# Three orders changed in a two-layer MLP behind a Fourier layer: weight sums by a written plan, output sums over three iterations, VectorE's PSUM sums first

## The chip, the cores and the metric

The kernel runs on one core of a Trainium2 chip. The metric is the device time in microseconds (us). The engines are TensorE (PE, with PEld for its weight loads), VectorE (DVE), ScalarE (ACT), GpSimd (POOL) and SyncE (SP), whose queue issues the transfers that matter here. Each engine takes its own instructions in program order; semaphores order the engines against one another.

## The reference

A Fourier layer gives 6016 tokens of 256 numbers; two MLP layers follow, and their weights are `moe_` and `moe2_`:

```python
def reference(...):
    x = attn_out.reshape(B * S, D)          # rfft, complex matmul, soft threshold, irfft
    h = x @ w_in;  g = h * (1.0 / (1.0 + np.exp(-h)));  x = g @ w_out      # layer 1, d_ff 2048
    h = x @ w_in2; g = np.maximum(0.01 * h, h);         return g @ w_out2  # layer 2
```

## The kernel before

Numbers are float32, and TensorE works on rounded ones, so each operand is split: ScalarE copies the *high* part, VectorE or GpSimd subtracts it from the source to get the *low* part, and one product is three matmuls (low weight x high data, high x low, high x high).

The MLP runs over 12 chunks of tokens (11 of 512, one of 384) for layer 1 and the same 12 for layer 2. Within a chunk, eight iterations take one pair of 128 hidden units each. An iteration of the main loop works on three pairs in turn: `pr` (its first matmul), `one` (the pair before: its activation's parts are made) and `two` (the pair before that: its products with `w_out` are added up in PSUM, in four banks `acc(0)` to `acc(3)`).

Most pairs run "in blocks", a seven-product scheme for a 2x2 block product in place of eight. It needs sums of weight blocks, and sums of data blocks: `t1` (GpSimd), `t23` and `t4` (VectorE) make sums of the activation. The parts are `"1"` (`high`: h, `low`: l), `"a"` (ha, la; la on GpSimd) and `"b"` (hb, lb). At the end of a chunk the four banks are summed into two output tiles (`close`, or `finish` outside the quick chunks) and stored by SP. The first layer has the scheme for `w_out` only. In layer 2 the chunks 2 to 10 are *quick*: there the product with `w_in` too has seven products (`seven(k)`, three matmuls of 256 columns each), whose results `keep`, `join(0)` and `join(1)` put together in PSUM (px and py, four banks in turn, two per iteration). A quick iteration has 42 matmuls of 256 columns; `quick_turn` writes out its order by hand. The data sums of the next quick chunk (tsum, and the parts B11, B21, T1 to T4, B22) are made one step an iteration, from the third on (`ahead_quick`, `make_next`); in the last iteration of a chunk two steps are made.

Between the layers, weights are exchanged. The last chunk of layer 1 (the short one) and the chunks 0 and 1 of layer 2 are the 24 iterations that are called *the tail* here, numbered 0 to 23 from the variable `tail`. In them, `next_in` splits `w_in` of layer 2 for each pair, `sums_w2` makes four sums of `w_out` blocks a pair on GpSimd (128x128 each), which `split_w` splits in the next iteration, and `sum_in` takes three iterations a pair: GpSimd adds the high and low parts of `w_in` together again (128x512), VectorE makes four sums of 128x128, and then the sums are split. Three lists of iterations say when:

```python
SEVENS_AT = [9, 12, 15, 16, 17, 18, 19, 20]
IN_AT, SUMS_AT = [1, 3, 4, 6, 7, 9, 10, 12], [3, 5, 6, 8, 10, 11, 13, 14]
```

All of this stands at the end of the iteration, after `one.high("b")` and `one.low("b")`. In a quick iteration VectorE's order is t23, t4, low "1", join 0, join 1, (closing sums), low "b".

Of the kernel before, what the change touches and what calls it, by code (L numbers as in the profile page):

```python
# [9 lines left out]
F32 = mybir.dt.float32  # L10
F32R = mybir.dt.float32r
# [69 lines left out]
def spectral_mlp_kernel(ctx, tc, x, w_r, w_i, b_r, b_i, w_in1, w_out1, w_in2, w_out2, da, ea, dm, out):  # L81
# [349 lines left out]
    big = pool("big", 1, side="right", **near)  # L431
    m4 = pool("m4", 2, side="right", **near)
    ring = [big.tile([128, 2, RING], F32R, name=f"x{p}") for p in parts]
    place = lambda layer, c: CHUNKS[c][0] % RING if layer == 1 or c < 2 else 512
    at = lambda t: t % RING
    quick = lambda layer, c: layer == 2 and 2 <= c < len(CHUNKS) - 1
    accs, x2f, late = {}, {}, {}

    def inverse(h, c):
# [44 lines left out]
    def sum_x2(c, second):  # L484
        x = [x2f[c][h][:, t * 256:(t + 1) * 256] for h in range(2) for t in range(2)]
        if not second:
            sums_x[c] = [stage.tile([128, 512], F32, tag="wraw", name="tsum", bufs=2) for _ in range(2)]
        t1, t2, t3, t4 = (u[:, k * 256:(k + 1) * 256] for u in sums_x[c] for k in range(2))
        for d, a, b in ((t2, x[3], t1), (t4, x[2], t2)) if second else ((t1, x[1], x[0]), (t3, x[3], x[1])):
            nc.gpsimd.tensor_tensor(out=d, in0=a, in1=b, op=ALU.subtract)  # L490

# [7 lines left out]

    def ahead_quick(c):  # L500
        pool_, x = nc.gpsimd, lambda h, a, b: x2f[c][h][:, a:b]
        return [[lambda: load_x2(c)], [],
                [lambda: sum_x2(c, False), lambda: split_b(c, B22, 1, x(1, 256, 512), pool_)],
                [lambda: sum_x2(c, True)],
                [lambda: split_b(c, T1, 2, sums_x[c][0], pool_), lambda: split_b(c, T3, 2, sums_x[c][1], nc.vector)],
                [lambda: [split_b(c, k, 1, x(h, 0, 256)) for h, k in enumerate((B11, B21))]],
                [lambda: [split_b(c, k, 1, x(h, 0, 256), nc.vector, False) for h, k in enumerate((B11, B21))]]]

    made = [0]

# [45 lines left out]
    def sums_w2(p):
        sums_w(p, m_out[p // 4][:, p % 4 * 512:][:, :512])

    def next_in(p):

        src, hi, lo = (w[:, :, p % 4 * 256:][:, :, :256] for w in [m_in[p // 4]] + [w_in[p // 4][q] for q in parts])
        nc.scalar.copy(hi, src)
        nc.vector.tensor_tensor(out=lo, in0=src, in1=hi.bitcast(F32), op=ALU.subtract)

    sums_in = []

    def sum_in(p):
        if p % 4 == 0:
            sums_in.append({q: homes[p // 4].tile([128, 4, 4, 128], F32R, tag=f"hold{k}", name=f"s{q}") for k, q in enumerate(parts)})
        t = btp.tile([128, 1024], F32, tag="bt", name="wsum")  # L570
        r, s = t[:, :512].rearrange("p (h e) -> p h e", h=2), t[:, 512:].rearrange("p (i e) -> p i e", i=4)
        hi, lo = (w_in[p // 4][q][:, :, p % 4 * 256:][:, :, :256].bitcast(F32) for q in parts)
        nc.gpsimd.tensor_tensor(out=r, in0=hi, in1=lo, op=ALU.add)
        yield
        a = [r[:, h, u * 128:(u + 1) * 128] for u in range(2) for h in range(2)]
        for d, x, y, op in ((s[:, 0], a[2], a[3], ALU.add), (s[:, 2], a[0], a[2], ALU.subtract),
                            (s[:, 1], s[:, 0], a[0], ALU.subtract), (s[:, 3], a[1], s[:, 1], ALU.subtract)):
            nc.vector.tensor_tensor(out=d, in0=x, in1=y, op=op)  # L578
        yield
        hi, lo = (sums_in[p // 4][q][:, p % 4] for q in parts)  # L580
        nc.scalar.copy(hi, s)  # L581
        nc.vector.tensor_tensor(out=lo, in0=s, in1=hi.bitcast(F32), op=ALU.subtract)

    class Pair:

# [156 lines left out]
                    self.product(self.acc(i)[:, :self.n], wh[w], wl[w], hi, lo, b, e)  # L742

        def close(self):
            if self.p != NF // 2 - 1:
                return [lambda: None] * 4
            tt, g = nc.vector.tensor_tensor, nc.gpsimd.tensor_tensor
            half = lambda a, k: a[:, k * 256:(k + 1) * 256]
            both = lambda a: a.rearrange("p (k n) -> p k n", k=2)
            twice = lambda a: a.rearrange("p (k n) -> p k n", k=1).to_broadcast([128, 2, 256])  # L750
            acc = [self.acc(i) for i in range(4)]
            o = [stage.tile([128, 512], F32, tag="wraw", name="x2o", bufs=2) for _ in range(2)]
            u = stage.tile([128, 256], F32, tag="wc", bufs=4, name="u")
# [9 lines left out]
            def third():
                nc.scalar.copy(u, half(acc[2], 0))
                tt(out=half(o[0], 1), in0=half(o[0], 1), in1=half(acc[2], 0), op=ALU.add)
                tt(out=u, in0=u, in1=half(acc[2], 1), op=ALU.add)

            def fourth():
                tt(out=half(o[1], 1), in0=half(o[1], 1), in1=half(acc[3], 0), op=ALU.subtract)
                g(out=half(o[0], 0), in0=half(o[0], 0), in1=u, op=ALU.add)  # L770
                g(out=both(o[1]), in0=both(o[1]), in1=twice(u), op=ALU.add)
# [3 lines left out]
            return [first, second, third, fourth]  # L775

        def finish(self, part):
            if self.p != NF // 2 - 1:
# [52 lines left out]
    SEVENS_AT = [9, 12, 15, 16, 17, 18, 19, 20]  # L831
    IN_AT, SUMS_AT = [1, 3, 4, 6, 7, 9, 10, 12], [3, 5, 6, 8, 10, 11, 13, 14]

    def make_next():
        if todo and (make := todo.pop(0)):
            make()

    sevens = []

    def quick_turn(pr, one, two, i):  # L840
        last = pr.p == NF // 2 - 1
        if pr.p == 2:
# [36 lines left out]
        sp[6]()
        pr.seven(4)  # L880
        pr.unit(0)
        pr.t1()
        closing[2]()
        closing[3]()
        if not last:
            make_next()

    for i in range(len(pairs) + 2):
# [74 lines left out]
        if k <= i <= NF:  # L963
            split_w()
            if i < NF:
                sums_w1(i - k)
        elif i < tail:
            if i == NF + 1:
                for home in homes:
                    m_in.append(home.tile([128, DFF], F32, tag="hold0", name="m_in").rearrange("p (d c) -> p d c", d=2))  # L970
                    m_out.append(home.tile([128, DFF], F32, tag="hold1", name="m_out"))
                _, step_w, _, _ = weight_pieces(w_in2, w_out2, lambda k: [m_in[k]], lambda k: [m_out[k]], 1)
            if i > NF and i % 2 == 0:
                step_w()
        else:
            split_w()
            if i - tail in IN_AT:
                next_in(IN_AT.index(i - tail))
            if i - tail in SUMS_AT:
                sums_w2(SUMS_AT.index(i - tail))  # L980
            if i - tail in SEVENS_AT:
                sevens.append(sum_in(SEVENS_AT.index(i - tail)))
            for steps in list(sevens):
                if next(steps, sevens) is sevens:
                    sevens.remove(steps)


# [25 lines left out]
```

## Time and profile before

| | |
|---|---|
| median of 3 runs | 1172.87 us (1170.99 to 1173.26) |
| profiled execution | 1171.28 us, span 1169.5 us |
| granted TensorE clock | 1.000 of full speed |
| busy share of the span | PE 98%, PEld 91%, DVE 71%, ACT 72%, POOL 55% |

The span runs from the first to the last instruction; about 1.8 us of the profiled time lie around it. Busy shares are averages over stages that have different limits, so the stages are to be read one by one.

### The profile page before, as it was taken

How to read it: one execution, taken by the hardware profiler on the slowest of the kernel's cores; microseconds unless marked ns; L12 is line 12 of the kernel's file. 1: busy time of each engine (PE TensorE's matmuls, PEld its weight loads, DVE VectorE, ACT ScalarE, POOL GpSimd, SP SyncE). 2: the span in 40 equal slices, each digit the busy share in tenths (PEclk: the TensorE clock that was granted, in tenths of full speed). 3: DMA queues.
4: the chain of work that ended last, by engine and by line, in shares of the span. 5: the costliest groups of instructions: out<-in, count | busy, mean ns of one | idle time of the engine just before them, and what ended most of it. 6: DMA issues, size and time to landing. Idle time of an engine off the chain costs nothing.

```text
span 1169.5 us, 21790 instructions
## 1 busy us (share of the span) xinstructions
PE 1140.8 (98%) x7932; PEld 1062.5 (91%) x7932; DVE 835.2 (71%) x1543; ACT 843.9 (72%) x1801; POOL 638.9 (55%) x693
## 2 busy tenths in 40 slices
PE   9999999999999999999999988789999999999998
PEld 9889988889999999999999976689999999999998
DVE  4898865455666666666665688888788778877863
ACT  4788876666666666667666765578888888888884
POOL 0567746444454454544544675546756665666552
PEclk9999999999999999999999999999999999999999
DMA  9345532010111210111100001010111011001000
GB/s 245 115 135 160 166 122 91 14 50 19 57 53 41 64 59 28 59 50 35 46 29 27 17 26 36 1 37 2 37 37 37 2 37 37 13 25 38 32 3 31
DMA packets 36187, 61.84 MB, mean 53 GB/s; under 512 B 3952, under 2 KB 16080, under 8 KB 36080
## 3 DMA queue, kind: packets, MB, share of 16 engines
q1 hardware_dynamic: 35792, 60.28, 16.5%
q8 instruction: 62, 1.02, 0.3%
q14 instruction: 45, 0.37, 0.1%
q10 hardware_dynamic: 288, 0.18, 0.1%
HBM read 41.83 MB, written 18.61 MB: 52 GB/s over the span
## 4 chain that ended last, share of the span: by engine, by line
PE 79%; DVE 12%; ACT 4%; issue 3%; POOL 2%; DVEq 0%; POOLq 0%
PE acc L709 30%; PE ph L636 24%; PE px L612 6%; PE pz L332 6%; PE py L612 4%; PE py L361 3%; PE pa L284 3%; PE px L446 2%; DVE u L683 2%; DVE wsum L578 2%; PE pb L384 1%; DVE l L664 1%; DVE lb L664 1%; DVE u L621 1%; DVE u L690 1%
## 5 line engine op out<-in xcount | busy, mean ns | idle before, releaser
L664 POOL TENSOR_TENSOR la<-u,ha 128x512 fp32r<-128x512 f32 (+1 forms) x176 | 226.2, 1286 | 172.9 <-ACT ha L702 172.9
L664 DVE TENSOR_TENSOR lb<-u,hb 128x768 fp32r<-128x768 f32 (+1 forms) x176 | 177.1, 1006 | 155.5 <-ACT hb L702 155.3
L676 POOL TENSOR_TENSOR u<-u 128x256 f32<-128x256 f32 x160 | 139.4, 871 | 84.5 <-ACT u L627 61.5
L702 ACT CAST hb<-u 128x768 fp32r<-128x768 f32 (+1 forms) x176 | 141.8, 806 | 59.1 <-DVE u L690 58.1
L636 PE MATMUL ph<-xhi,winhi 128*128 128x512 f32 (+1 forms) x480 | 143.6, 379 | 0.0
L636 PE MATMUL ph<-xlo,winhi 128*128 128x512 f32 (+1 forms) x480 | 143.4, 379 | 0.0
L636 PE MATMUL ph<-xhi,winlo 128*128 128x512 f32 (+1 forms) x480 | 143.2, 379 | 0.0
L709 PE MATMUL acc<-lb,whi 128*128 128x256 f32 (+1 forms) x496 | 138.6, 279 | 4.6 <-DVE lb L664 4.6
L709 PE MATMUL acc<-hb,wlo 128*128 128x256 f32 (+1 forms) x496 | 137.8, 278 | 0.0
L709 PE MATMUL acc<-hb,whi 128*128 128x256 f32 (+1 forms) x496 | 137.6, 277 | 0.0
L702 ACT CAST ha<-u 128x512 fp32r<-128x512 f32 (+1 forms) x176 | 110.8, 629 | 2.1 <-PE acc L709 1.9
L659 ACT ACTIVATE ph<-ph 128x512 f32<-128x512 f32 (+1 forms) x112 | 64.7, 577 | 63.8 <-PE ph L636 63.8
L709 PE MATMUL acc<-l,whi 128*128 128x256 f32 (+1 forms) x336 | 94.3, 281 | 11.0 <-DVE l L664 11.0
L636 PEld LDWEIGHTS ph<-xhi,winhi 128*128 128x128 f32 x480 | 89.5, 187 | 15.9
L636 PEld LDWEIGHTS ph<-xlo,winhi 128*128 128x128 f32 x480 | 89.4, 187 | 15.7
L709 PE MATMUL acc<-ha,wlo 128*128 128x256 f32 (+1 forms) x352 | 99.3, 282 | 0.5 <-ACT shi L581 0.4
L709 PEld LDWEIGHTS acc<-lb,whi 128*128 128x128 f32 x496 | 93.1, 188 | 6.3 <-DVE lb L664 6.3
L709 PE MATMUL acc<-la,whi 128*128 128x256 f32 (+1 forms) x352 | 98.8, 281 | 0.0
L709 PE MATMUL acc<-ha,whi 128*128 128x256 f32 (+1 forms) x352 | 98.7, 280 | 0.0
L709 PE MATMUL acc<-h,wlo 128*128 128x256 f32 (+1 forms) x336 | 94.9, 282 | 1.6 <-ACT x2o L785 1.6
L659 ACT ACTIVATE u<-ph 128x512 f32<-128x512 f32 (+1 forms) x80 | 47.0, 588 | 67.0 <-PE ph L636 65.1
L683 DVE TENSOR_TENSOR u<-px,u 128x512 f32<-128x512 f32 x72 | 49.7, 690 | 63.7 <-ACT h L702 42.2
(176 smaller groups left out, 3584.0 us busy)
## 6 DMA issues: line engine op xcount, KB each, us to landing
wraw<-in_moe_w_in_dram SPq DMA_DIRECT2D x32, 256.0 KB
wraw<-in_moe_w_out_dram SPq DMA_DIRECT2D x32, 256.0 KB
scr<-bo SPq DMA_DIRECT2D x48, 128.0 KB
scr<-x2o SPq DMA_DIRECT2D x22, 256.0 KB
x2i<-scr SPq DMA_DIRECT2D x22, 256.0 KB
out_dram<-x2o SPq DMA_DIRECT2D x22, 256.0 KB
dmr<-in_dm_dram SPq DMA_DIRECT2D x34, 160.0 KB
bt<-scr SPq DMA_DIRECT2D x14, 384.0 KB
```

Source lines behind the costliest of these rows:

```text
L284: nc.tensor.matmul(pa[h][:, s * 128:(s + 1) * 128], lhsT=xt[c][:, s, h * 128:(h + 1) * 128], rhs=da_sb, start=True, stop=True, skip_group_ ...
L332: nc.tensor.matmul(turned(pz), lhsT=u[:, h, :], rhs=turned(v[:, h].rearrange("p g e -> p (g e)")), start=(n == 0), stop=(n == len(terms) - 1))
L361: nc.tensor.matmul(turned(py), lhsT=u, rhs=turned(v), start=False, stop=(n == len(terms) - 1), skip_group_check=True)
L446: nc.tensor.matmul(px[:, s * PAIR:(s + 1) * PAIR], lhsT=bt[:, s, h * 128:(h + 1) * 128], rhs=ea_sb, start=True, stop=True, skip_group_chec ...
L612: nc.tensor.matmul(turned(out), lhsT=x, rhs=turned(y), start=(k < 3 and i == 0), stop=(i == 2), skip_group_check=True)
L636: nc.tensor.matmul(turned(ph), lhsT=u[:, h, f % HALF * 128:][:, :128], rhs=turned(v[:, h, :]), start=(i == 0), stop=(i == len(terms) - 1))
L659: nc.scalar.activation(out=out, in_=ph, func=ACTF.Silu)
L664: eng.tensor_tensor(out=lo, in0=src, in1=hi.bitcast(F32), op=ALU.subtract)
L676: nc.gpsimd.tensor_tensor(out=blk(1), in0=blk(0), in1=blk(2), op=ALU.subtract)
L683: nc.vector.tensor_tensor(out=v[:, 3:5], in0=b22, in1=v[:, 0:2], op=ALU.subtract)
L702: nc.scalar.copy(hi, src)
L709: nc.tensor.matmul(turned(dst), lhsT=u, rhs=turned(v), start=(begin and self.p == 0 and i == 0), stop=(end and self.p == NF // 2 - 1 and i ...
```

## The change

- The weight exchange follows one table, `PLAN`: generators that do a step each time they are called, with the iterations (from -6 to 23) in which they step. `sums_w2`, `next_in` and `sum_in` take two pairs at once (256 columns an instruction where there were 128). `sum_in` reads the unsplit weights `m_in`, makes all its sums on GpSimd, and the splits follow later in `split_in`. `plan` is called behind the products and ahead of `one.high("b")`.
- `close` has seven parts in place of four: one ScalarE copy more (both halves of `acc(2)`), VectorE adds two PSUM halves fewer into other tiles, GpSimd has two sums more; and the parts are spread over iterations 1, 2 and 3 of the next chunk, with the store at the end of iteration 3.
- In `quick_turn`, `one.low("1")` goes behind `join(0)` and `join(1)`; the order of `two`'s products that was used in the closing iteration is now used in all.
- In `ahead_quick`, T1 to T4 are split one by one (256 columns), T1 and T3 an iteration earlier; in a chunk's last iteration B11 is made (both parts) behind `keep(2)`, ahead of `high("a")`, and B21 behind `join(1)`, ahead of `low("1")`.

```diff
     def sum_x2(c, second):
...
-            sums_x[c] = [stage.tile([128, 512], F32, tag="wraw", name="tsum", bufs=2) for _ in range(2)]
+            sums_x[c] = [stage.tile([128, 256], F32, tag="wc", name="tsum", bufs=4) for _ in range(4)]
...
     def ahead_quick(c):
...
+        t = lambda k, eng: split_b(c, k, 1, sums_x[c][k - T1], eng)
         return [[lambda: load_x2(c)], [],
                 [lambda: sum_x2(c, False), lambda: split_b(c, B22, 1, x(1, 256, 512), pool_)],
-                [lambda: sum_x2(c, True)],
-                [lambda: split_b(c, T1, 2, sums_x[c][0], pool_), lambda: split_b(c, T3, 2, sums_x[c][1], nc.vector)],
-                [lambda: [split_b(c, k, 1, x(h, 0, 256)) for h, k in enumerate((B11, B21))]],
-                [lambda: [split_b(c, k, 1, x(h, 0, 256), nc.vector, False) for h, k in enumerate((B11, B21))]]]
+                [lambda: sum_x2(c, True), lambda: t(T1, pool_), lambda: t(T3, nc.vector)],
+                [lambda: t(T2, pool_), lambda: t(T4, nc.vector)],
+                [lambda: split_b(c, B11, 1, x(0, 0, 256), nc.vector)], [lambda: split_b(c, B21, 1, x(1, 0, 256), nc.vector)]]
...
+    def sums_w2(k):
+        b = m_out[k // 2][:, k % 2 * 1024:][:, :1024].rearrange("p (j i e) -> p i j e", j=2, i=4)
...
+            nc.gpsimd.tensor_tensor(out=d, in0=x, in1=y, op=op)
+            yield
...
+        for i, n, u in ((A11, 1, src[:, :, :1]), (A12, 2, src[:, :, 2:]), (S1, 2, t[0]), (S3, 2, t[1])):
+            hi, lo = (late[q][:, 2 * k:2 * k + 2, i:i + n] for q in parts)
+            nc.scalar.copy(hi, u)
+            nc.vector.tensor_tensor(out=lo, in0=u, in1=hi.bitcast(F32), op=ALU.subtract)
+            yield
...
+    def sum_in(k):
+        src = m_in[k // 2][:, :, k % 2 * 512:][:, :, :512].rearrange("p h (j u e) -> p j u h e", j=2, u=2)
...
+            nc.gpsimd.tensor_tensor(out=d, in0=x, in1=y, op=op)
+            yield
...
+            return [first, second, third, fifth, fourth, sixth, seventh]
...
+    PLAN = [(sum_in(0), [-6, -5, -4, -1]), (sums_w2(0), [-3, -3, -2, -2, 3, 3, 4, 4]), (sum_in(1), [0, 1, 2, 3]),
+            (next_in(0), [1, 2]), (sums_w2(1), [5, 5, 6, 6, 6, 6, 7, 7]), (next_in(1), [4, 5]),
+            (sums_w2(2), [8, 8, 9, 9, 9, 9, 10, 10]), (next_in(2), [8, 9]), (sums_w2(3), [11, 11, 12, 12, 12, 12, 13, 13]),
+            (next_in(3), [10, 11]), (split_in(0), [14, 15]), (split_in(1), [15, 16]), (sum_in(2), [16, 17, 18, 19]),
+            (sum_in(3), [17, 18, 19, 20]), (split_in(2), [21, 21]), (split_in(3), [22, 23])]
...
         one.t4()
+        close(2)
         pr.keep(2)
-        one.low("1")
+        if last:
+            make_next()
         one.high("a")
         one.low("a", nc.gpsimd)
         sp[0]()
         sp[1]()
-        closing[0]()
         pr.seven(6)
         pr.keep(1)
-        if last:
-            make_next()
+        close(1)
+        close(2)
...
         pr.seven(7)
         pr.join(1)
-        closing[1]()
         if last:
             make_next()
+        one.low("1")
+        close(1)
+        close(1)
         one.low("b")
...
         pr.t1()
-        closing[2]()
-        closing[3]()
+        close(2)
+        close(3)
         if not last:
             make_next()
...
+        plan(i - tail)
         if one:
             one.high("b")
             one.low("b")
```

## Rows read from the trace of the kernel before

**Rows 1.** The page's first part: busy time, share, instructions by engine.

```profile
PE 1140.8 (98%) x7932; PEld 1062.5 (91%) x7932; DVE 835.2 (71%) x1543; ACT 843.9 (72%) x1801; POOL 638.9 (55%) x693
```

**Rows 2.** Busy time in stretches: layer 1, the tail's second part, quick chunks.

```profile
473.20:508.90 35.70, 35.70 (x233) 32.52 (x232) 23.26 (x41) 24.37 (x46) 16.99 (x18) 1.00 0.10 33
...
691.40:766.80 75.40, 56.52 (x333) 47.28 (x331) 66.74 (x99) 39.51 (x77) 43.01 (x45) 1.00 0.04 15
766.80:1127.90 361.10, 355.97 (x3023) 351.19 (x3024) 291.24 (x503) 305.02 (x645) 227.32 (x212) 1.00 0.08 27
```

**Rows 3.** The same for one quick chunk, and its iterations 0, 1, 2, 3, 7.

```profile
806.96:846.97 40.01, 39.43 (x337) 38.86 (x336) 32.34 (x57) 34.00 (x72) 25.59 (x24) 1.00 0.08 28
806.96:811.79 4.83, 4.83 (x44) 4.83 (x43) 4.71 (x8) 3.91 (x8) 2.14 (x3) 1.00 0.01 3
811.79:816.78 4.99, 4.99 (x45) 4.88 (x43) 3.64 (x8) 4.79 (x11) 2.30 (x3) 1.00 0.01 2
816.78:822.36 5.58, 5.07 (x44) 4.87 (x43) 5.55 (x11) 4.04 (x9) 3.99 (x5) 1.00 0.21 82
822.36:827.18 4.82, 4.82 (x44) 4.82 (x43) 3.82 (x7) 3.90 (x8) 2.66 (x3) 1.00 0.42 126
...
841.69:847.08 5.39, 5.32 (x44) 5.07 (x43) 4.19 (x9) 5.17 (x12) 4.11 (x4) 1.00 0.00 0
```

**Rows 4.** Waits in the stretch 686 to 767 us, by total.

```profile
ACT hb L702 <- DVE u L690: 35.9, 11, 6.2
...
PE acc L709 <- DVE l L664: 11.0, 6, 2.9
```

**Rows 5.** VectorE's groups by shape, 686 to 767 us.

```profile
L578 DVE TENSOR_TENSOR wsum<-wsum 128x128 f32<-128x128 f32 x28 | 24.4, 912 | 0.2
```

**Rows 6.** Timeline of VectorE in the tail: one sum alone.

```profile
741.83 0.29 DVE L578 TENSOR_TENSOR wsum<-wsum 128x128 f32<-128x128 f32 x1
```

**Rows 7.** GpSimd's groups by shape, 600 to 1130 us.

```profile
L664 POOL TENSOR_TENSOR la<-u,ha 128x512 fp32r<-128x512 f32 x95 | 123.3, 1298 | 90.2 <-ACT ha L702 90.2
...
L490 POOL TENSOR_TENSOR tsum<-x2i,tsum 128x256 f32<-128x256 f32 x18 | 13.3, 738 | 0.7
```

**Rows 8.** VectorE's timeline in iteration 0 of that quick chunk.

```profile
808.61 0.69 DVE L683 TENSOR_TENSOR u<-px,u 128x512 f32<-128x512 f32 x1
809.34 0.42 DVE L690 TENSOR_TENSOR u<-u,px 128x256 f32<-128x256 f32 x1
809.67 0.68 DVE L664 TENSOR_TENSOR l<-px,h 128x512 fp32r<-128x512 f32 x1
810.27 0.68 DVE L621 TENSOR_TENSOR u<-py,qr 128x512 f32<-128x512 f32 x1
810.87 0.42 DVE L623 TENSOR_TENSOR px<-px,qr 128x256 f32<-128x256 f32 x1
811.21 0.95 DVE L664 TENSOR_TENSOR lb<-u,hb 128x768 fp32r<-128x768 f32 x1
```

**Rows 9.** ScalarE's timeline in the same iteration.

```profile
808.65 0.66 ACT L702 CAST ha<-u 128x512 fp32r<-128x512 f32 x1
...
810.99 0.63 ACT L627 ACTIVATE u<-u 128x512 f32<-128x512 f32 x1 [0.35 <-DVE u L621]
```

**Rows 10.** TensorE's timeline there: last matmul of seven(7).

```profile
810.28 0.27 PE L612 MATMUL px<-xhi,shi 128*128 128x256 f32 x1
```

**Rows 11.** VectorE's timeline in iterations 1 to 2: closing sums, then t23.

```profile
816.82 1.45 DVE L664 TENSOR_TENSOR lb<-u,hb 128x768 fp32r<-128x768 f32 x1
818.20 0.41 DVE L765 TENSOR_TENSOR x2o<-x2o,acc 128x256 f32<-128x256 f32 x1
...
819.19 0.68 DVE L683 TENSOR_TENSOR u<-px,u 128x512 f32<-128x512 f32 x1
```

**Rows 12.** GpSimd's timeline there: t1 beside lb.

```profile
816.73 0.73 POOL L676 TENSOR_TENSOR u<-u 128x256 f32<-128x256 f32 x1 [1.22 <-ACT u L627]
```

**Rows 13.** VectorE's quick-stretch groups by shape: splits of 256 columns.

```profile
L498 DVE TENSOR_TENSOR xlo<-x2i,xhi 128x256 fp32r<-128x256 f32 x17 | 6.4, 416 | 0.0
```

More of the change, by code (lines that the diff above doesn't have):

```diff
@@ L32 @@
 KT = 14
+QUICK = 2
 def turned(a):
@@ L433, in spectral_mlp_kernel @@
     ring = [big.tile([128, 2, RING], F32R, name=f"x{p}") for p in parts]
-    place = lambda layer, c: CHUNKS[c][0] % RING if layer == 1 or c < 2 else 512
+    place = lambda layer, c: CHUNKS[c][0] % RING if layer == 1 or c < QUICK else 512
     at = lambda t: t % RING
-    quick = lambda layer, c: layer == 2 and 2 <= c < len(CHUNKS) - 1
+    quick = lambda layer, c: layer == 2 and QUICK <= c < len(CHUNKS) - 1
     accs, x2f, late = {}, {}, {}
@@ L486, in sum_x2 @@
         if not second:
-            sums_x[c] = [stage.tile([128, 512], F32, tag="wraw", name="tsum", bufs=2) for _ in range(2)]
-        t1, t2, t3, t4 = (u[:, k * 256:(k + 1) * 256] for u in sums_x[c] for k in range(2))
+            sums_x[c] = [stage.tile([128, 256], F32, tag="wc", name="tsum", bufs=4) for _ in range(4)]
+        t1, t2, t3, t4 = sums_x[c]
         for d, a, b in ((t2, x[3], t1), (t4, x[2], t2)) if second else ((t1, x[1], x[0]), (t3, x[3], x[1])):
@@ L554, in sums_w1 @@
         sums_w(p, r)
[L556 to L582, printed above, removed]
@@ new lines, in sums_w2 @@
+    def sums_w2(k):
+        b = m_out[k // 2][:, k % 2 * 1024:][:, :1024].rearrange("p (j i e) -> p i j e", j=2, i=4)
+        b = [b[:, i] for i in range(4)]
+        t = [stage.tile([128, 2, 2, 128], F32, tag="wraw", name="wsum", bufs=2) for _ in range(2)]
+        s1, s2, s3, s4 = (u[:, :, i] for u in t for i in range(2))
+        for d, x, y, op in ((s1, b[1], b[3], ALU.add), (s3, b[0], b[1], ALU.subtract),
+                            (s2, s1, b[0], ALU.subtract), (s4, b[2], s2, ALU.subtract)):
+            nc.gpsimd.tensor_tensor(out=d, in0=x, in1=y, op=op)
+            yield
+        src = m_out[k // 2][:, k % 2 * 1024:][:, :1024].rearrange("p (j i e) -> p j i e", j=2, i=4)
+        for i, n, u in ((A11, 1, src[:, :, :1]), (A12, 2, src[:, :, 2:]), (S1, 2, t[0]), (S3, 2, t[1])):
[3 more added lines that the diff above has]
+            yield
@@ new lines, in next_in @@
+    def next_in(k):
+        src, hi, lo = (w[:, :, k % 2 * 512:][:, :, :512] for w in [m_in[k // 2]] + [w_in[k // 2][q] for q in parts])
+        for h in range(2):
+            nc.scalar.copy(hi[:, h], src[:, h])
+            nc.vector.tensor_tensor(out=lo[:, h], in0=src[:, h], in1=hi[:, h].bitcast(F32), op=ALU.subtract)
+            yield
+    sums_in, sums_src = [], []
+    def sum_in(k):
+        src = m_in[k // 2][:, :, k % 2 * 512:][:, :, :512].rearrange("p h (j u e) -> p j u h e", j=2, u=2)
+        t = btp.tile([128, 2, 4, 128], F32, tag="bt", name="wsum")
+        sums_src.append(t)
+        a = [src[:, :, u, h] for u in range(2) for h in range(2)]
+        s = [t[:, :, i] for i in range(4)]
+        for d, x, y, op in ((s[0], a[2], a[3], ALU.add), (s[2], a[0], a[2], ALU.subtract),
+                            (s[1], s[0], a[0], ALU.subtract), (s[3], a[1], s[1], ALU.subtract)):
+            nc.gpsimd.tensor_tensor(out=d, in0=x, in1=y, op=op)
+            yield
@@ new lines, in split_in @@
+    def split_in(k):
+        if k % 2 == 0:
+            sums_in.append({q: homes[k // 2].tile([128, 4, 4, 128], F32R, tag=f"hold{n}", name=f"s{q}") for n, q in enumerate(parts)})
+        t = sums_src.pop(0).rearrange("p j i e -> p j (i e)")
+        for j in range(2):
+            hi, lo = (sums_in[k // 2][q][:, k % 2 * 2 + j].rearrange("p i e -> p (i e)") for q in parts)
+            nc.scalar.copy(hi, t[:, j])
+            nc.vector.tensor_tensor(out=lo, in0=t[:, j], in1=hi.bitcast(F32), op=ALU.subtract)
+            yield
@@ L752, in close @@
             o = [stage.tile([128, 512], F32, tag="wraw", name="x2o", bufs=2) for _ in range(2)]
-            u = stage.tile([128, 256], F32, tag="wc", bufs=4, name="u")
+            w = []
             def first():
@@ L759, in second, with third, fifth, sixth @@
                 nc.scalar.copy(both(o[1]), twice(half(acc[1], 1)))
+            def third():
                 for i in range(2):
                     tt(out=half(o[i], 0), in0=half(o[i], 0), in1=half(acc[1], 0), op=ALU.add)
[L763 to L766, printed above, removed]
             def fourth():
+                w.extend(stage.tile([128, 256], F32, tag="wc", bufs=4, name="u") for _ in range(2))
+                for k in range(2):
+                    nc.scalar.copy(w[k], half(acc[2], k))
+            def fifth():
                 tt(out=half(o[1], 1), in0=half(o[1], 1), in1=half(acc[3], 0), op=ALU.subtract)
-                g(out=half(o[0], 0), in0=half(o[0], 0), in1=u, op=ALU.add)
-                g(out=both(o[1]), in0=both(o[1]), in1=twice(u), op=ALU.add)
+            def sixth():
+                g(out=half(o[0], 1), in0=half(o[0], 1), in1=w[0], op=ALU.add)
+                g(out=w[0], in0=w[0], in1=w[1], op=ALU.add)
+            def seventh():
+                g(out=half(o[0], 0), in0=half(o[0], 0), in1=w[0], op=ALU.add)
+                g(out=both(o[1]), in0=both(o[1]), in1=twice(w[0]), op=ALU.add)
                 for h in range(2):
                     nc.sync.dma_start(out=out[:, h, self.t0:self.t0 + self.n], in_=o[h])
-            return [first, second, third, fourth]
+            return [first, second, third, fifth, fourth, sixth, seventh]
         def finish(self, part):
@@ L829, in spectral_mlp_kernel, with plan @@
     blocks = lambda i: pairs[i] if 0 <= i < len(pairs) and pairs[i].mode != "plain" else None
-    SEVENS_AT = [9, 12, 15, 16, 17, 18, 19, 20]
-    IN_AT, SUMS_AT = [1, 3, 4, 6, 7, 9, 10, 12], [3, 5, 6, 8, 10, 11, 13, 14]
+    PLAN = [(sum_in(0), [-6, -5, -4, -1]), (sums_w2(0), [-3, -3, -2, -2, 3, 3, 4, 4]), (sum_in(1), [0, 1, 2, 3]),
[3 more added lines that the diff above has]
+            (sum_in(3), [17, 18, 19, 20]), (split_in(2), [21, 21]), (split_in(3), [22, 23])]
+    def plan(i):
+        for steps, when in PLAN:
+            for _ in range(when.count(i)):
+                next(steps)
     def make_next():
@@ L836, in make_next @@
             make()
-    sevens = []
+    closing = []
     def quick_turn(pr, one, two, i):
@@ L843, in quick_turn, with close @@
             todo[:] = ahead(*phases[phases.index((pr.layer, pr.c)) + 1])
-        sp, closing = two.steps(), two.close()
+        sp = two.steps()
         if two.p == NF // 2 - 1:
-            sp = [sp[k] for k in (0, 1, 2, 4, 3, 5, 6)]
+            closing[:] = two.close()
+        sp = [sp[k] for k in (0, 1, 2, 4, 3, 5, 6)]
+        def close(p):
+            if pr.p == p and closing:
+                closing.pop(0)()
         for k in (1, 2, 5):
@@ L974, in spectral_mlp_kernel @@
                 step_w()
[L975 to L985, printed above, removed]
 _INS = ["x", "w_r", "w_i", "b_r", "b_i", "moe_w_in", "moe_w_out", "moe2_w_in", "moe2_w_out"]
```

2 lines of the change are left out of this document (removed).

## Prediction

> **What bounds the kernel now.** I read the page's first part, then the stretches, then waits and timelines of the bad ones. TensorE is busy 98% of the span [rows 1], so time can come only from stretches in which it falls behind its own pace. In layer 1, 35.7 us hold seven iterations, 5.10 each, with TensorE busy throughout [rows 2]: that is its pace there. The ten iterations 14 to 23 of the tail take 75.4 us for the same 33 matmuls each, and TensorE is busy for 56.5 while VectorE is busy for 66.7 of them [rows 2]. The waits say who is late: TensorE waits 11.0 us for l, and ScalarE 35.9 us for u of VectorE [rows 4]. VectorE's costliest group there is the 128x128 sums: 28 of them, 912 ns on average [rows 5], though one alone takes 0.29 [rows 6]. At 5.10 the ten iterations would take 51.0: **24.4 us are lost in the tail.**
>
> The quick chunks fill 361.1 us [rows 2]. One takes 40.0, an undisturbed iteration 4.83, which is 42 matmuls of 0.115 [rows 3]. Over that lie iteration 1 by 0.16, 2 by 0.75 and 7 by 0.56 [rows 3]. Iterations 1 and 2 carry the closing sums of the chunk before: three of them stand behind lb on VectorE and push t23 to 819.19, 2.4 us into its iteration [rows 3, 11], against 1.65 in iteration 0 [rows 8]. Iteration 7 carries the splits of the next data.
>
> **Why sums are dear on VectorE.** t1 on GpSimd runs from 816.73 to 817.46, and lb, which starts at 816.82 and has both inputs in SBUF, takes 1.45 in place of 0.95 and ends 0.81 after t1 [rows 8, 11, 12]. So the second waits for the whole of the first, though some 0.15 of its fixed cost is spent meanwhile. Operations with an input in PSUM keep their 0.68 beside la [rows 8]. The Trainium skill (SBUF — State Buffer, "Who interferes with whom") states that rule: a VectorE instruction with two SBUF inputs and a GpSimd one that reads SBUF exclude each other. By that rule, the trace agrees.
>
> **The change in the tail.** Removed from VectorE: 32 sums, some 28 us with their waiting [rows 5]. GpSimd loses 32 sums of 128 columns and the eight additions of 512, and gets 32 sums of 256, strided. No row has that shape; the nearest is 0.74 for 256 columns, and the bounds are 0.74 and the 1.30 of 512 [rows 7]. I take 0.74, since the column count is the same: 23.7 us, about what goes. VectorE keeps the splits in wider pieces: 28 of 512 columns at about 0.69 (the 512-column durations of [rows 8]) and 4 of 256 at 0.42 [rows 13], 21 us over 23 iterations. It spends 2.75 of each 5.10 on its regular work (0.69, 0.42, 0.68, 0.96, [rows 8]), so up to three pieces fit in an iteration, and the plan never has more.
>
> What remains is the exclusion. Iteration 12 has la 1.30, t1 0.74, two sums 1.48, a data split 1.30, lb 0.96 and two splits 1.1: 6.9 us that exclude each other, in 5.10. Iterations 11 and 13 have 5.2 and 5.7, 14 has 3.7. Who has waited is 0.15 shorter, and the backlog stays under 2.5 us. It is covered because parts made in an iteration are used in the next: lb, if it ends 7.1 us after its iteration's start, is needed for the products of "b" at 5.1 + 4.1 = 9.2. I walked the queues of 24 iterations in program order with these durations: in the old order this gives 76 us for the ten iterations (75.4 in [rows 2]), in the new one no wait of TensorE. One step could hurt: in iteration 3 the first splits write weights that the same iteration's products still read, and hb stands behind them; that costs hb 1.3 us, inside the same slack. **Tail: -24.4 us**, with 5 less if a sum costs 1.30 (the same walk).
>
> **The change at a chunk's start.** The first two copies stay in iteration 1; VectorE has three sums of 0.41 where it had five, two of them behind low "1" in iteration 1 and one in iteration 2 ahead of join(0). t23 of iteration 2 starts at 1.7 and not 2.4. ScalarE's two copies of `acc(2)` end 3.25 us into iteration 2; their products begin at 3.4 at the earliest: close, 0.1 if missed. GpSimd's two sums more and the later store hide in iterations 2 and 3: la's result is needed 2.2 us into the next iteration, and GpSimd has 2.0 regular of 4.83. The store now goes behind the load of the next chunk's data on SP, so that load waits for nothing new; nobody waits for the store before the next chunk's closing. Gain 0.16 + 0.75 - 0.0: **nine closings, -8.2 us** (-6 if 0.25 stays).
>
> **The change in every quick iteration.** join(0) can start when seven(3) is done, about 2.95 after the start, join(1) when seven(7) is: its last matmul starts at 810.28 and lasts 0.27 [rows 10], so 3.64 from 806.96, with 0.05 for the way (an estimate). Low "1" follows at 3.99 and ends at 4.68. It now reads px just before seven(1) of the next pair writes the same bank, which is four tiles, two iterations, further on. From join(1)'s end at 811.29 [rows 8] to the next pair at 811.79 [rows 3] are 0.50, of which seven(4)'s matmuls are 0.345; the 0.155 left is the way from VectorE's end to a matmul. So seven(1) can start at 4.84, against 4.83 now: the wait of seven(4) on join(1) goes, one of the same size on low "1" takes its place. **72 iterations, 0** (0 to +3).
>
> **The change at a chunk's end.** T1 to T4 are spread better, but VectorE's splits of T3 and T4 stand among GpSimd's work. unit 0 now ends at 4.3 and t1 follows at 4.4 (before: unit 0 ended at 811.62, 4.66 [rows 9]), ahead of lb at 4.6, so lb waits and ends at 5.9 to 6.0. In iteration 6 the split of T4 comes behind lb and behind GpSimd's T2, and ends 2.05 into iteration 7. t23, t4 follow, and B11's low part is ready to start at 3.05. But la starts at 2.71 (ha is put off 0.3 by B11's copy) and holds the port to 4.0. B11's low part ends at 4.27, then join(0) 4.87, join(1) 5.21, B21 5.55, low "1" 6.15, and seven(1) of the next chunk starts at 6.30: iteration 7 loses 1.5 us, against 0.56 before. If B11 gets in ahead of la, join(1) ends at 4.05, B21 at 4.4, low "1" at 5.0: it loses 0.35. With t23 on time B11 would be ready at 2.69 against la's 2.71, so an on-time t23 is needed; I take the blocked case. **Eight such iterations, +7.5 us** (-1.7 in the other).
>
> **Sum.** 1171.28 of the profiled execution (1169.5 span and 1.8 around it) - 24.4 - 8.2 + 0 + 7.5 = 1146.2. That execution is 1.6 below the median of the runs shown; I add half of this: **1147 us**.
>
> **Rivals.**
> *B11 first.* t1 and lb change places in iteration 6 if unit 0 is 0.1 later there, T4's split ends early, and B11 beats la. For it: the margin is 0.1 in a walk that meets the old iterations to 0.1. Against: every earlier iteration has t1 first. 1147 - 9.2 = 1138.
> *GpSimd binds in the tail.* The sums cost near 1.30, or TensorE waits on the exclusion: +5, up to +10 with doubled waits, 1152 to 1157. Against: GpSimd's total work doesn't grow. The Trainium skill (GPSIMD Engine Reference, "Engine selection") bids elementwise work with two inputs go to VectorE, GpSimd being about twice as slow; unblocked rows agree (0.42 against 0.74), but here VectorE's sums were not unblocked.
> *Slower: low "1" holds the next pair.* seven(1) waits for low "1" in all 72 iterations. The walk has 0.01 per iteration; from 0.36 on (1172.9 - 1147 over 72), the rest as forecast, the kernel is slower. It would need join(1) to start at 4.0, not 3.65, say by ScalarE's third copy for join(0) slipping 0.5 behind ha: 0.45 each gives 1179. Against: ha ends at 809.31, 2.35 in [rows 9], and that copy is the next.
> *It doesn't do what it says.* VectorE stays the bound in the tail because its splits now wait for GpSimd as its sums did, and the closings gain nothing while iteration 7 loses: with all 24 lost still, 1172 to 1179. Little speaks for it: 32 blocked operations are gone.
>
> **Chances.** Forecast (iteration 7 blocked, tail clear) 0.58, 1143 to 1151; B11 first 0.19, 1134 to 1142; GpSimd binds 0.15, 1151 to 1159; low "1" holds 0.05; no effect 0.03, which counts as same for the most part. Eight in ten, reaching into the second and third: 1135 to 1156. Under 0.2%, some 2.3 us, a measurement can't tell a change from none. Faster 0.93, same 0.02, slower 0.05.
>
> **What would show it.** Right: iterations 14 to 23 at 5.1 each with no 128-column sum on VectorE; iterations 1 and 2 of a quick chunk at 4.83 to 4.95; iteration 7 near 6.3, with a low-part split of about 1.2 us on VectorE beside la. Wrong: waits of TensorE on l in every quick iteration; iterations of the tail above 5.5; iteration 7 near 5.2 (then the time is some 9 us lower); GpSimd's new sums well above 0.74 where no VectorE operation holds them.

## The result, and the profile after

The changed kernel takes 1139.74 us (median of 4 runs, 1139.07 to 1140.31), the kernel before 1171.93 in the runs beside it: a ratio of 0.9725, 95% interval 0.9708 to 0.9742. The time lies in the range, 7.3 us below the forecast.

The page of the changed kernel, its first part and the first line of the chain that ended last:

```profile
PE 1129.0 (99%) x7932; PEld 1058.6 (93%) x7932; DVE 840.1 (74%) x1486; ACT 846.4 (74%) x1812; POOL 661.5 (58%) x712
...
PE 98%; DVE 1%; issue 0%; DMA 0%; SPq 0%; ACT 0%; DVEq 0%
```

Against [rows 1], the span fell by 31.8 us (1169.5 to 1137.7) with as many matmuls, and TensorE's busy share rose to 99%: waits went. The busy time in stretches (length; busy time and instructions of PE, PEld, DVE, ACT, POOL; granted clock; DMA): the tail's iterations 14 to 23, one quick chunk, its iterations 0, 1, 2, 3 and 7, and an iteration 7 of another chunk:

```profile
691.34:742.48 51.14, 51.14 (x333) 46.57 (x331) 38.33 (x60) 37.17 (x69) 36.71 (x38) 1.00 0.07 22
...
782.08:821.72 39.64, 39.03 (x338) 38.83 (x337) 36.19 (x56) 34.44 (x75) 27.98 (x28) 1.00 0.09 28
782.08:786.94 4.86, 4.86 (x45) 4.86 (x44) 4.36 (x8) 3.94 (x8) 2.28 (x3) 1.00 0.33 101
786.94:791.75 4.81, 4.81 (x45) 4.81 (x43) 4.09 (x7) 4.61 (x10) 1.66 (x2) 1.00 0.00 0
791.75:796.58 4.83, 4.83 (x44) 4.83 (x43) 4.80 (x10) 4.32 (x11) 2.33 (x3) 1.00 0.00 0
796.58:801.39 4.81, 4.81 (x44) 4.81 (x43) 4.16 (x7) 3.91 (x8) 4.18 (x5) 1.00 0.02 5
815.97:821.72 5.75, 5.14 (x44) 4.94 (x43) 5.72 (x9) 4.71 (x11) 3.25 (x4) 1.00 0.06 11
934.84:939.71 4.87, 4.87 (x45) 4.87 (x44) 4.83 (x9) 4.47 (x11) 4.20 (x5) 1.00 0.12 27
```

The tail takes 51.1 where it took 75.4 [rows 2], and VectorE is busy for 38.3 of it, not 66.7. Iterations 1 and 2 take 4.81 and 4.83 for 4.99 and 5.58 [rows 3]. Iteration 7 comes in two lengths: 5.75 in six of the eight chunks that have a quick one behind them, 4.87 in two. So the difference is 24.3 from the tail, 8.5 from the nine iterations 1 and 2 (44.9 to 43.3 and 50.3 to 43.4 us, each summed over the chunks), and a loss of 1.1 in iterations 7 (6 x 0.92 + 2 x 0.04 over 4.83, where before had 8 x 0.56): 31.7 of the 31.8.

VectorE's timeline of the changed kernel in a long iteration 7, from 776.33 on (start, duration):

```profile
777.51 0.96 DVE L499 TENSOR_TENSOR xlo<-tsum,xhi 128x256 fp32r<-128x256 f32 x1
778.39 0.68 DVE L703 TENSOR_TENSOR u<-px,u 128x512 f32<-128x512 f32 x1
779.10 0.42 DVE L710 TENSOR_TENSOR u<-u,px 128x256 f32<-128x256 f32 x1
779.44 1.19 DVE L499 TENSOR_TENSOR xlo<-x2i,xhi 128x256 fp32r<-128x256 f32 x1
780.55 0.68 DVE L641 TENSOR_TENSOR u<-py,qr 128x512 f32<-128x512 f32 x1
781.15 0.42 DVE L643 TENSOR_TENSOR px<-px,qr 128x256 f32<-128x256 f32 x1
781.49 0.41 DVE L499 TENSOR_TENSOR xlo<-x2i,xhi 128x256 fp32r<-128x256 f32 x1
781.82 0.68 DVE L684 TENSOR_TENSOR l<-px,h 128x512 fp32r<-128x512 f32 x1
```

GpSimd's and TensorE's timelines there (what a wait was for stands in brackets):

```profile
779.06 1.29 POOL L684 TENSOR_TENSOR la<-u,ha 128x512 fp32r<-128x512 f32 x1 [0.88 <-ACT ha L722]
```

```profile
781.62 0.38 PE L632 MATMUL px<-xhi,winlo 128*128 128x256 f32 x1 [0.62 <-DVE px L643]
...
782.08 0.28 PE L632 MATMUL px<-xhi,winlo 128*128 128x256 f32 x1
```

B11's low part starts 0.38 behind la and takes 1.19, as forecast, and all behind it on VectorE moves: join(1) ends at 781.57. But TensorE waits for join(1) alone (781.62 is seven(4)). seven(1) of the next pair starts at 782.08, while low "1" runs until 782.50. The same lines of the short iteration 7, which began at 934.84, VectorE and then GpSimd:

```profile
936.53 0.68 DVE L703 TENSOR_TENSOR u<-px,u 128x512 f32<-128x512 f32 x1
937.24 0.42 DVE L710 TENSOR_TENSOR u<-u,px 128x256 f32<-128x256 f32 x1
937.58 0.42 DVE L499 TENSOR_TENSOR xlo<-x2i,xhi 128x256 fp32r<-128x256 f32 x1
```

```profile
937.57 1.58 POOL L684 TENSOR_TENSOR la<-u,ha 128x512 fp32r<-128x512 f32 x1 [0.36 <-ACT ha L722]
```

Here t23 starts 1.69 into its iteration, not 2.06, and B11 goes first.

### The profile page after: what moved, and what is told of

Read it like the earlier page. It is cut to its first block, busy times and chain, and to the rows that moved or that the text cites. A ratio compares the mean times of both kernels' runs of the same rounds, so it can differ in the third digit from the quotient of the medians.

```text
span 1137.7 us, 21760 instructions
## 1 busy us (share of the span) xinstructions
PE 1129.0 (99%) x7932; PEld 1058.6 (93%) x7932; DVE 840.1 (74%) x1486; ACT 846.4 (74%) x1812; POOL 661.5 (58%) x712
## 4 chain that ended last, share of the span: by engine, by line
PE 98%; DVE 1%; issue 0%; DMA 0%; SPq 0%; ACT 0%; DVEq 0%
PE acc L729 40%; PE ph L656 28%; PE px L632 9%; PE py L632 7%; PE pz L333 6%; PE py L362 3%; PE px L447 2%; PE pa L285 2%; PE pb L385 1%; DMA xt<-in_x_dram 0%; DVE u L641 0%; DVE xlo L499 0%; DVE px L643 0%; SPq L262 0%; PE warm L273 0%
## 5 line engine op out<-in xcount | busy, mean ns | idle before, releaser
L684 POOL TENSOR_TENSOR la<-u,ha 128x512 fp32r<-128x512 f32 (+1 forms) x176 | 228.5, 1299 | 164.8 <-ACT ha L722 161.2
L684 DVE TENSOR_TENSOR lb<-u,hb 128x768 fp32r<-128x768 f32 (+1 forms) x176 | 197.4, 1121 | 136.9 <-ACT hb L722 136.8
L696 POOL TENSOR_TENSOR u<-u 128x256 f32<-128x256 f32 x160 | 120.9, 756 | 67.9 <-ACT u L647 44.7
L729 PE MATMUL acc<-h,whi 128*128 128x256 f32 (+1 forms) x336 | 93.7, 279 | 0.0
L729 PEld LDWEIGHTS acc<-hb,whi 128*128 128x128 f32 x496 | 93.2, 188 | 0.0
```

Of the source, the lines that this page charges most:

```text
L684: eng.tensor_tensor(out=lo, in0=src, in1=hi.bitcast(F32), op=ALU.subtract)
L696: nc.gpsimd.tensor_tensor(out=blk(1), in0=blk(0), in1=blk(2), op=ALU.subtract)
L729: nc.tensor.matmul(turned(dst), lhsT=u, rhs=turned(v), start=(begin and self.p == 0 and i == 0), stop=(end and self.p == NF // 2 - 1 and i ...
```

## Experiments

### The tail: plan, engine, times

**The plan alone.** The kernel before with `PLAN` and its generators; close, order and data splits as before.

> The kernel before with the tail's plan alone (sums_w2, next_in, sum_in, split_in, PLAN); quick chunks, closing and data splits as before. If the three parts of the change add up, the ten iterations 14 to 23 take 51 to 52 us in place of 75.4, the quick chunks stay at 40.0, and the time is 1171.9 - 24.3 = 1147.6 (1146 to 1149). If the tail's gain is tied to the new quick order (the data sums of the first quick chunk are made in the tail too), iterations 20 to 23 stay long and the time is above 1150.

1147.09 us (1146.75 to 1147.37), ratio 0.9788 (0.9773 to 0.9802): 24.6 less than before, as this part was forecast.

**The engine alone**, in the kernel before:

```diff
         for d, x, y, op in (...):
-            nc.vector.tensor_tensor(out=d, in0=x, in1=y, op=op)
+            nc.gpsimd.tensor_tensor(out=d, in0=x, in1=y, op=op)
```

> The kernel before with one word changed: the four 128-column sums of sum_in go from VectorE to GpSimd. Theory A (the engine: VectorE's sums waited for GpSimd, so taking them off VectorE is the gain): most of the 24 us come back, 1147 to 1153. Theory B (the plan: less work for a pair, made in wider pieces at other times): GpSimd then has la, t1, the addition of 512, four sums and the data sums in the same iterations, and a walk of the queues gives 66 to 67 us for the ten iterations in place of 76, so 1162 (1158 to 1166).

1163.91 us, ratio 0.993 (0.9914 to 0.9947): 8 of the 24. Its waits from 686 to 767 us (total, times, longest), and its iterations 14 to 23:

```profile
PEld acc L709 <- POOL la L664: 6.4, 2, 3.4
PE acc L709 <- POOL la L664: 6.0, 2, 3.2
...
691.55:757.65 66.10, 56.38 (x332) 49.45 (x330) 48.61 (x68) 38.51 (x75) 61.60 (x72) 0.95 0.05 17
```

TensorE now waits mostly for la, which stands behind the sums on GpSimd, in place of l [rows 4]; GpSimd is busy for 61.6 of the 66.1 us. The granted clock is 0.95 in this stretch, for 1.00 before, so up to some 3 us (an estimate: 0.05 of 66.1) of what is still lost can be the clock's.

**The reverse**, the changed kernel with the new sums on VectorE (one word in `sum_in`).

> The changed kernel with one word changed: sum_in's 16 sums of 256 columns go back to VectorE. Theory A: each waits for GpSimd's running instruction and holds up l and lb behind it, as before: 5 to 15 us lost, 1145 to 1155. Theory B: at one or two an iteration they fit into VectorE's free 2.3 us: 1139.7, no difference beyond 1 us.

1140.92 us (1140.03 to 1141.71), 1.2 above the changed kernel, where theory B allowed 1; the tail's iterations stay at 5.1. The costliest of its new sums among VectorE's groups, 600 to 743 us (busy, mean ns):

```profile
L591 DVE TENSOR_TENSOR wsum<-m_in 128x256 f32<-128x256 f32 x8 | 5.5, 698 | 0.0
```

Its profiled execution took 0.8 more than that of the changed kernel, which one more long iteration 7 covers (seven of eight here, 0.9 us).

**Neither engine nor times**: the fastest version (below), with the sums on VectorE and bunched.

```diff
-    PLAN = [(sum_in(0), [-6, -5, -4, -1]), ... (sum_in(1), [0, 1, 2, 3]),
+    PLAN = [(sum_in(0), [9, 9, 12, 12]), ... (sum_in(1), [13, 13, 14, 14]),
...
-            ... (split_in(0), [14, 15]), (split_in(1), [15, 16]), (sum_in(2), [16, 17, 18, 19]),
-            (sum_in(3), [17, 18, 19, 20]), (split_in(2), [21, 21]), (split_in(3), [22, 23])]
+            ... (split_in(0), [15, 15]), (split_in(1), [16, 16]), (sum_in(2), [17, 17, 18, 18]),
+            (sum_in(3), [19, 19, 20, 20]), (split_in(2), [21, 21]), (split_in(3), [22, 23])]
```

> The same run (1133.7) with the tail's output-side gains undone as far as engine and time go: sum_in's 16 sums of 256 columns run on VectorE again, and two at a time in the iterations 9 and 12 to 20, about where the kernel before made them. Theory A' (engine or early times are the gain, either being enough): the tail gets long again, 5 to 20 us, 1139 to 1154. Theory B' (the gain is that there is less to do: no adding together of high and low parts, 16 wide sums in place of 32, no chain of three iterations a pair): within 1.5 us, 1133 to 1135.5.

1134.14 us (1133.33 to 1134.92), as without the edit. Its stretch of iterations 14 to 23:

```profile
692.33:743.47 51.14, 51.14 (x332) 46.56 (x331) 44.69 (x73) 38.89 (x72) 31.74 (x31) 1.00 0.08 24
```

VectorE is busy for 6.4 us more than in the changed kernel, GpSimd for 5.0 less, TensorE all the time in both. So the gain needs neither the engine of these sums nor their dates. What the versions at 51.1 share is the rest of the plan: half as many sums of twice the width, no second addition of the parts, no chain of three iterations, `w_out`'s sums and splits two pairs at a time at new dates, and all of it ahead of `one.high("b")`. No run takes these apart.

### Iteration 7

**B11's low part behind the joins**, in the changed kernel, where B21's is made:

```diff
-                [lambda: split_b(c, B11, 1, x(0, 0, 256), nc.vector)], [lambda: split_b(c, B21, 1, x(1, 0, 256), nc.vector)]]
+                [lambda: split_b(c, B11, 1, x(0, 0, 256))],
+                [lambda: split_b(c, B11, 1, x(0, 0, 256), nc.vector, False), lambda: split_b(c, B21, 1, x(1, 0, 256), nc.vector)]]
```

> The changed kernel with the low part of B11 in a chunk's last iteration moved behind join(1), ahead of B21's (its high part stays where it is). Theory C (B11's low part waits for la on GpSimd and holds join(0) and join(1) up): iteration 7 falls from 5.75 to 4.8 to 4.9 in all chunks, six of eight gain 0.9: 1134.3 (1133 to 1136). Theory D (iteration 7 is long because VectorE and ScalarE have two splits more in it, wherever they stand): iteration 7 stays at 5.5 to 5.8, 1139 to 1140.

1133.68 us (1133.35 to 1134.18), ratio 0.9674 (0.9659 to 0.9688), 6.1 less than the changed kernel: the fastest version here. The chunk that starts at 820.17:

```profile
820.17:858.84 38.67, 38.67 (x338) 38.67 (x337) 35.24 (x56) 34.21 (x75) 27.79 (x27) 1.00 0.08 29
```

TensorE is busy throughout, and the eight iterations 7 take 4.87 to 4.89. B11's wait for la was the whole loss of 0.9.

**Low "1" put back**, in that version, ahead of the joins:

```diff
         pr.keep(2)
+        one.low("1")
...
-        one.low("1")
```

> The run with B11's low part behind the joins (1133.7), with low "1" back at its old place ahead of the joins. Theory P (the prediction's walk: the order of low "1" costs and gains nothing in an undisturbed iteration, and takes 0.6 us a chunk out of the way of the closing sums and of the data splits): iteration 2 goes to 5.1, 6 and 7 to 4.9, 1139.3 (1137 to 1141). Theory Q (the order is free, all of the closing's gain comes from spreading its parts): no change, 1133.7.

1139.49 us (1139.4 to 1139.64): its place is worth 5.8 us. Iterations 2, 6 and 7 of one chunk:

```profile
791.25:796.41 5.16, 5.04 (x44) 4.85 (x43) 5.13 (x9) 4.38 (x11) 2.12 (x3) 1.00 0.00 0
811.32:816.25 4.93, 4.93 (x44) 4.93 (x43) 4.24 (x8) 4.37 (x11) 4.58 (x6) 1.00 0.01 3
816.25:821.22 4.97, 4.97 (x44) 4.90 (x43) 4.45 (x9) 4.75 (x12) 3.31 (x4) 1.00 0.00 0
```

Its waits from 743 to 1092 us:

```profile
PEld px L633 <- DVE px L644: 3.0, 10, 0.3
```

Where t23 is late, behind closing sums, low "1" passes that on to join(1), and seven(4) waits: nine of these ten waits stand in the nine iterations 2. The 0.1 more in iterations 6 and 7 shows no wait in the trace.

**The closing put back** to four parts, in the same version (the code of `close` and its four calls as before).

> The same run (1133.7) with the closing of the kernel before: four parts, all in iteration 1, the old copies and sums; low "1" stays behind the joins. Theory P: iterations 1 and 2 go to 4.95 to 5.0 each, not to the old 5.58, since with low "1" out of the way the joins come early even behind the closing sums: +0.4 us a chunk, 1137 (1136 to 1139). Theory Q: the whole 0.9 us a chunk comes back: 1141.8 (1141 to 1143).

1136.67 us (1136.3 to 1137.06): worth 3.0, in iterations 1 and 2. Two of them, first an iteration 2, then the iteration 1 ahead of it:

```profile
791.00:795.98 4.98, 4.98 (x44) 4.87 (x43) 4.95 (x11) 3.93 (x9) 3.43 (x4) 1.00 0.14 53
786.01:791.00 4.99, 4.99 (x44) 4.88 (x43) 4.15 (x7) 4.79 (x11) 1.73 (x3) 1.00 0.00 0
```

### Which bank low "1" holds

**Low "1" behind low "b"**, still in that version; by the prediction's step, seven(1) of the next pair must then wait in each iteration.

```diff
-        one.low("1")
         close(1)
         close(1)
         one.low("b")
+        one.low("1")
```

> The same run with low "1" moved still further back, behind low "b", so that it ends 1.0 to 1.5 us later in each iteration. The prediction's step (the next pair's first product writes the PSUM bank that low "1" reads, so it waits for it): TensorE waits over 1 us in all 72 quick iterations, above 1210 us. Its rival, as the trace after suggests (the next pair's px lies in another bank): only the products that use the low part "1" wait, where it is late, in iterations 0 and 2: 2.5 us a chunk at most, 1134 to 1157.

1152.74 us in one run, where the prediction's step asked for over 1210. Its waits from 743 to 1092 us:

```profile
PEld acc L730 <- DVE l L685: 18.1, 17, 1.3
PE acc L730 <- DVE l L685: 14.7, 17, 1.1
```

TensorE waits for l where it is used (the products with `w_out`, L730), 17 times, in iterations 0 and 2. At L633, seven(k), there is no wait for l. The programs as built list the bank of each tile; a few pairs in a row:

```
kernel before    px 0 1 2 3 0 1 2 3    py 2 3 0 1 2 3 0 1
kernel changed   px 0 1 3 0 1 3 0 1    py 2 2 2 2 2 2 2 2
```

In the kernel before a pair's py takes the bank of the px before last, and low "1" is that px's last reader: there seven(2), which opens py, would wait for a late low "1", and not seven(1), which opens px. In the changed kernel py has a bank of its own and three banks serve px, so the next pair waits for low "1" with neither. So the bank that the prediction counts on, px of the next pair, is shared in neither kernel. Of the versions here, those with low "1" ahead of join(0) have the first pattern, those with it behind have the second: py's last read, join(0), now comes first.

To force the sharing that the prediction has, two runs hold the four tiles and give them to even and odd pairs:

```diff
-                self.px, self.py = (ps_h.tile(...) for q in ("px", "py"))
+                if len(banks) < 4:
+                    banks.extend(ps_h.tile(...) for q in ("px", "py"))
+                self.px, self.py = banks[self.p % 2 * 2:][:2]
```

In the changed kernel ("the two-bank run"):

> The changed kernel with px and py of the quick pairs held in four fixed tiles, two for even and two for odd pairs, so that px of the next pair is the tile that low "1" reads; nothing else differs. Theory S (the prediction's step failed because in the changed kernel the next pair's px lies elsewhere: the list of allocations of the built program gives px the banks 0, 1, 3 in turn and py always bank 2; with the bank shared, seven(1) does wait for low "1"): steady iterations stay at 4.8, since low "1" ends 0.17 us ahead of the next seven(1) there; the iterations 7 grow by 0.5 to 0.75 us each (in the changed kernel low "1" ends 0.42 us behind the start of the next seven(1), and 0.155 is the way), some 5 us in all: 1143 to 1146.5 us. Theory N (a matmul that opens a bank is not held by a read of it, or the loss was limited elsewhere): 1139.7 us, within 1.

1141.32 us median of 4, from 1139.73 to 1143.87: the median lies between the two expected ranges, and the time alone says little. The profiled run is the one of 1143.87, so what its trace shows holds for that execution. Two of its iterations 7, and TensorE's timeline at the end of the first:

```profile
776.22:782.44 6.22, 5.23 (x44) 4.83 (x42) 6.19 (x10) 4.98 (x12) 3.73 (x4) 1.00 0.12 31
...
856.50:861.76 5.26, 5.01 (x44) 4.82 (x42) 5.13 (x10) 4.76 (x13) 4.38 (x4) 1.00 0.17 50
```

```profile
781.52 0.38 PE L636 MATMUL px<-xhi,winlo 128*128 128x256 f32 x1 [0.68 <-DVE px L647]
...
782.44 0.38 PE L636 MATMUL px<-xhi,winlo 128*128 128x256 f32 x1 [0.32 <-DVE l L688]
```

The second wait is the one that the prediction put there: seven(1) stands 0.32 us for l. Six of the eight iterations 7 are of the long kind, 6.22 for 5.75, the two short ones 5.3 for 4.87. The iteration 0 behind them takes 4.9 (once 5.15), and nearly all others stay at 4.8 to 4.9.

In the version with low "1" behind low "b":

> The kernel with B11's low part and low "1" both put back (low "1" behind low "b"), with the same four fixed tiles for px and py. Without them it took 1152.7 us, and low "1" ended some 0.45 us behind the start of the next seven(1) in its steady iterations. Theory S: every quick iteration waits for low "1", 0.6 us or more each and more where lb is held by GpSimd: 1185 to 1225 us, with waits of TensorE for l at its px matmuls. Theory N: 1152.7 us, within 3.

1239.16 us in one run, 86 more and above what was expected. Its waits from 743 to 1092 us, and the busy time from 743 to 1200, in one iteration 0, in half a microsecond of it and in an iteration 4:

```profile
PEld px L637 <- DVE l L689: 61.4, 54, 2.4
PE px L637 <- DVE l L689: 50.7, 54, 2.2
...
743.00:1200.00 457.00, 390.80 (x3057) 376.66 (x3056) 292.76 (x496) 322.63 (x676) 240.83 (x239) 0.95 0.06 21
790.91:798.20 7.29, 6.67 (x43) 6.47 (x43) 3.69 (x6) 3.97 (x8) 2.57 (x2) 0.77 0.08 30
792.40:792.90 0.50, 0.50 (x4) 0.50 (x4) 0.39 (x1) 0.50 (x3) 0.00 (x0) 0.50 0.00 0
818.36:824.02 5.66, 5.08 (x42) 4.88 (x42) 3.62 (x6) 4.23 (x9) 4.23 (x5) 1.00 0.25 94
```

54 times, in nearly every iteration, seven(k) now waits for l. A part of the 86 us is the clock's: it was granted in full up to 743 us, and in 13 of the next 71 iterations its mean is 0.76 or 0.77. TensorE is busy for 6.65 us in these and for 5.09 in the others, so some 20 us are the clock's (an estimate: 13 times the difference). A shared bank does hold seven(1), and the changed kernel has none there.

## Why the prediction was right in direction and 7 us too high

**The tail**, -24.4: measured -24.3, with the plan alone -24.6. One reading was a little off: the last 1.5 of the 75.4 us already lie in the first quick iteration, which starts at 765.28 and stands for a data part on VectorE:

```profile
766.83 0.38 PE L612 MATMUL px<-xlo,winhi 128*128 128x256 f32 x1 [1.16 <-DVE xlo L498]
```

That loss has gone too (the first quick iteration took 6.34, now 4.81). The new sums cost GpSimd 0.73 when nothing holds them, as taken. A line of its groups in the changed kernel, 600 to 1130 us (durations in ns: least, median, most):

```profile
L591 POOL TENSOR_TENSOR wsum<-m_in x8: 730/734/1460, 601.6 to 718.8; 128x256 f32<-128x256 f32 x8
```

What was named as the cause, sums dear on VectorE beside GpSimd, is not needed for the gain: in the bunched run they cost 0.76 on average on VectorE (12.1 us for 16), against 0.42 for 256 columns that nothing holds [rows 13], and the tail stays at 5.1. The runs fit an engine that had more work than time: VectorE before, busy (waits for GpSimd included) for 66.7 us where TensorE's pace leaves 51.0 [rows 2], and GpSimd in the engine-alone run, busy for 61.6 of 66.1. With the plan VectorE has 44.7 at most (the bunched run). What the wider instructions, the work left out, the place in the iteration and the new dates each give is open.

**The closings**, -8.2: measured -8.5, but not all through the closing. Putting it back costs 3.0, putting low "1" back costs 5.8, of which 3.2 in iterations 2. Each put back alone loses about 3 of the 8.5; the other 2 are lost only with both as before, which no run has by itself. The prediction booked the sum under the spread of `close` and 0 for low "1"; in steady iterations that 0 is right, in iterations with a late t23 it isn't.

**The chunk's end**, +7.5: measured +1.1. This is the term that was mis-sized, and the step that failed is "It now reads px just before seven(1) of the next pair writes the same bank". The times ahead of that step were met: B11's low part at 3.11 to 4.30 (forecast 3.05 to 4.27), join(1)'s end at 5.24 (5.21), low "1"'s end at 6.17 (6.15). What failed is the bank: seven(1) opens px, and px of the next pair lies in another bank than the one low "1" reads, in both kernels. In the changed one low "1" ends 0.42 behind the start of seven(1), and nobody waits for it. With px's bank shared by force the iteration takes 6.22, against 6.30 forecast; as built it is 5.75. The forecast put the loss at 1.5 and it is 0.92: 0.58 in each of eight iterations, 4.6 us in all, of which the two-bank run shows 0.47 each. Had the banks stayed as in the kernel before, seven(2) would have waited some 0.2 (an estimate: low "1" ends at 6.17, seven(2) starts at 5.75 + 0.35, and 0.155 is the way); no run has that. The other 1.8 are the rival "B11 first": it came true in two of eight chunks (4.87, where the forecast blocks all).

**The rest.** The sum on the profiled execution is then 1171.28 - 24.3 - 8.5 + 1.1 = 1139.6, and that execution took 1139.5. The 0.8 added for the median wasn't needed. The median lies in the bracket that was given to "B11 first" (1134 to 1142), but for the most part by luck: that rival gives 1.8 of the 7.3 us, the bank 4.6. Of the other rivals: GpSimd did not bind in the tail (no iteration above 5.2), and low "1" holds the next pair only when a bank is shared.

What goes with 5.75 or 4.87 is seen one iteration earlier, where the rival "B11 first" put it: at the end of iteration 6 lb and t1 become ready almost together. VectorE and GpSimd there in a chunk with a short iteration 7, then the same two in a chunk with a long one:

```profile
1052.35 0.95 DVE L684 TENSOR_TENSOR lb<-u,hb 128x768 fp32r<-128x768 f32 x1
```

```profile
1052.36 1.53 POOL L696 TENSOR_TENSOR u<-u 128x256 f32<-128x256 f32 x1
```

```profile
776.07 1.51 DVE L684 TENSOR_TENSOR lb<-u,hb 128x768 fp32r<-128x768 f32 x1
```

```profile
776.04 0.73 POOL L696 TENSOR_TENSOR u<-u 128x256 f32<-128x256 f32 x1
```

In the other short one, which began at 934.84, lb went first in iteration 6 too (934.59 against 934.86) and already in iteration 5. In the changed kernel, the reverse run and the two-bank run, the profiles have 18 chunks with t1 first in iteration 6, all with a long iteration 7, and six with lb first, five of them short. The sixth (two-bank run, t23 at 1.75) is long, because la starts 0.07 ahead of B11. So the order in iteration 6 goes with the length, but no run forced it; the two-bank run's spread of 4 us would fit a varying number of short iterations, and was not taken apart either.

## What to carry to other kernels

Before costing a wait on a tile that is handed on, look up in the built program which buffer the next owner gets, and do it again after a move: moving a tile's last reader can change who inherits it. Here the wrong bank was worth 0.47 us in an iteration 7. An operation that can be held by another engine belongs behind those on which TensorE waits, not ahead: moving one low part back by two places gave 6.1 us. Where an engine is behind in a stretch, compare its work with the time first: the new plan (half as many sums, wider, among other things) took the whole loss away on either engine, while the engine alone gave 8 of 24 us.

## What was not expected of the hardware

The order in which VectorE and GpSimd take turns hangs on very little: lb at 1052.35 went ahead of t1 at 1052.36, and in the short iteration B11's low part, shown at 937.58, took 0.42 while la, shown at 937.57, took 1.58 in place of 1.30. So within one execution the same iteration of the program came out at 5.75 in six chunks and at 4.87 in two. A sum of 256 strided columns took GpSimd 0.73, no more than one of 256 contiguous ones [rows 7]. In the run with the shared bank and low "1" behind low "b", TensorE stood for 1.79 us ahead of the iteration that starts at 790.91, and within that iteration its granted clock was at the lower level, 0.50 of full speed (1.2 GHz), from 792.3 to 795.6. All 13 iterations with such a stretch come right behind a stand of 1.8 or 2.2 us, though not every such stand was followed by one; the iterations whose longest stand was some 0.6 us kept 1.00.
